# Attention, then two MLPs, in one kernel: q, k and v loaded by whole tiles of tokens, and the attention weights transposed in quarters of the array

## The chip, the cores and the metric

The kernel runs on one core of one Trainium2 chip. The metric is device time in microseconds (us), as the median of several runs. The profile is of one execution.

## The reference

For 8 batches, 8 heads, 576 tokens and a head dimension of 64, attention is computed inside chunks of 64 tokens: scores = q k^T / 8, a softmax over the 64 keys of the chunk, times v. The result, 4608 tokens by 512, goes through two MLPs one after the other:

```python
out = np.matmul(attn, v_c)                     # per (batch, head, chunk of 64 tokens)
x = out.transpose(0, 2, 1, 3).reshape(B * S, H * D)      # 4608 x 512
r = np.maximum(x @ w_in1, 0.0);  x = (r * r) @ w_out1    # 512 -> 2048 -> 512
h = x @ w_in2
g = np.where(h >= 1, h, np.where(h <= -1, 0.0, (h + 1) ** 2 / 4))
return (g @ w_out2).astype(np.float32)
```

q, k and v are float32, the four weight matrices float64.

## The kernel before, in words

A *tile of tokens* is 128 tokens, two chunks; there are 36. A *unit* is half of a tile's heads (HU = 4 heads, as NP = 2 pairs); there are 72 units, two to a tile (UT = 2). The steps of a unit u are functions of their own:

- `load_qk(u)` loads q and k of the unit into one `qkn`, from four buffers in turn (QB = 4). A tile that straddles two batches (4 of 36) needs two DMAs where others need one. `load_v(t)` loads v of a whole tile into one of two `vt` with four DMAs: for each chunk c, the even and the odd heads separately, so that the keys of even heads lie on partitions 0 to 63 and those of odd heads on 64 to 127.
- `att_a` transposes q and k on TensorE into `psA` (four 128x128 transposes), `att_ae` copies them to `qkT` on ScalarE.
- `att_b` makes the scores in `psB`, eight 64x64 matmuls. Rows of the array follow the head's parity e, output partitions follow the chunk c, and the two parities write into two banks of PSUM. Then VectorE takes the row maxima `m` and multiplies them by minus the scale. `att_exp` is four activations on ScalarE with that bias and scale; they also sum up into `z`. `att_n` inverts `z` on VectorE and multiplies on GpSimd.
- `att_c` transposes the weights `s` into `psC` (two 128x128 transposes), `att_ce` copies them to `atT` on ScalarE.
- `att_d` multiplies with v into `psD`, eight 64x64 matmuls whose rows and whose output partitions both follow e, so two quarters of the array are used. `att_x` splits the result into a high part `xh` (ScalarE) and the rest `xl` (VectorE), each in two pieces of 64 partitions.

A float32 matmul stands in the profile as two records (eight matmuls are 16), a float32 transpose as one.

The order of every engine is written out by hand. The *head* is 11 turns, `head(i)`, in which TensorE does attention only: unit i's `att_a`, unit i-1's `att_b`, i-2's `att_c`, i-3's `att_d`. In the turns of DEC a piece of `w_in1` is decoded from float64 as well (`decode`, with `stage_piece` as its load and `bits`, `piece_a` to `piece_c`). After the head, slots follow: `plain_h`, the first matmul of MLP 1 (`ph`), takes 288 slots of six 128x512 matmuls each, and a turn of attention is spread over four slots: `att_d`, `att_b` and `att_x` behind the first, `att_exp` behind the second, `att_c`, `att_ce` and `att_n` behind the third, `att_a`, `att_ae` and the loads behind the fourth. Each two slots yield a `g`, which GpSimd squares and the SP queue stores in two DMAs. Beside this the other three weight matrices are decoded, in 48 units of one per 5.1 slots (`stage_unit`, `unit_a` to `unit_d`): two loads and two stores for most of them, and four sums on GpSimd (`sums`), so that a block of weights becomes the seven combinations of Strassen's method (`wd`, index CIDX). All DMAs are issued by SP, in the program's order.

From slot 288 on come three stretches of 280 slots with the remaining matrix products (`form_b`, `form_a`, line L454 of `products`). The last 16 units of weights are finished there (`late_a` to `late_d`).

Of the kernel before, what the change touches and what calls it, by code (L numbers as in the profile page):

```python
# [15 lines left out]
P = 128  # L16

TINY = 2.0**-15 * 1.125
CH = 64
# [7 lines left out]
CIDX = {"P4": 0, "P1": 1, "P2": 2, "P5": 3, "P6": 4, "P7": 5, "P3": 6}  # L27
# [4 lines left out]
def chunk_attention_moe_moe2(ctx, tc, q, k, v, w_in1, w_out1, w_in2, w_out2, out):  # L32
# [125 lines left out]
    def stage_unit(m, a, b):  # L158
        t = ep.tile([P, 4 * P, 2], U32, tag="ws", name="wu", bufs=2)
        w = (w_out1, w_in2, w_out2)[m]  # L160
        if m == 1:
            src = w.rearrange("(kh kt p) f -> kt p kh f", kh=2, kt=2)[b]
            cols = [(a + fh * HF) * 2 * P for fh in (1, 0)]
        else:
            src = w.rearrange("(kh kk p) d -> kk p kh d", kh=2, kk=HF)[a]
            cols = [(2 * dh + b) * 2 * P for dh in (1, 0)]
        for i, c in enumerate(cols):
            nc.sync.dma_start(
                out=t[:, 2 * i * P:2 * (i + 1) * P].rearrange("p (h f) w -> p h (f w)", h=2),
                in_=src[:, :, c:c + 2 * P],  # L170
            )
        wst[m, a, b] = t
# [8 lines left out]
    def sums(c):  # L181

        for o, x, z, op in ((4, 0, 1, ALU.add), (6, 2, 0, ALU.subtract), (5, 4, 2, ALU.subtract), (7, 3, 5, ALU.subtract)):
            nc.gpsimd.tensor_tensor(out=c[:, o], in0=c[:, x], in1=c[:, z], op=op)
# [5 lines left out]
    def unit_b(m, a, b):  # L190
        y, ab = wst[m, a, b]
        if m == 2:
            c = ep.tile([P, 4, P], F32, tag="wl", name="wq", bufs=2, padded_shape=[P, 7, P])
        else:
            c = ep.tile([P, 8, P], F32, tag="wc", name="wc", bufs=1)
# [10 lines left out]
    def unit_c(*u):  # L206
        c = wst[u]
        hi = ep.tile([P, 7, P], F32R, tag="wh", name="wh", bufs=2)
        nc.scalar.copy(hi, c[:, 1:8])
        wst[u] = (c, hi)  # L210
# [4 lines left out]
    def unit_d(m, a, b):  # L215
        c, hi = wst.pop((m, a, b))
        lo = ep.tile([P, 7, P], F32R, tag="wl", name="wl", bufs=2)
        nc.vector.tensor_tensor(out=lo, in0=c[:, 1:8], in1=f(hi), op=ALU.subtract)
        nc.sync.dma_start(out=wd[m, a][:, 1, b], in_=f(lo))


    def late_a(a, b):
        c = mp.tile([P, 8, P], F32, tag=f"q{LATE[0]}", name="lc")
# [6 lines left out]
    def late_c(a, b):  # L230
        c = wst[a, b]
        hi = mp.tile([P, 7, P], F32R, tag=f"q{LATE[1]}", name="lh", padded_shape=[P, 8, P])
        nc.scalar.copy(hi, c[:, 1:8])
        wst[a, b] = (c, hi)

    def late_d(a, b):
        c, hi = wst.pop((a, b))
        nc.gpsimd.tensor_tensor(out=c[:, 1:8], in0=c[:, 1:8], in1=f(hi), op=ALU.subtract)
        store_parts(2, a, b, hi, c[:, 1:8])
# [27 lines left out]
    def load_qk(u):  # L267
        runs, h0 = runs_of(u // UT), u % UT * HU
        qkn = rt(u % QB, [P, 2, HU, D], "qkn", padded=[P, 2, HU, D])
        for i, src in enumerate((q, k)):  # L270
            for r, n, b, s in runs:
                nc.sync.dma_start(
                    out=qkn[r:r + n, i],
                    in_=src[b, h0:h0 + HU, s:s + n, :].rearrange("h s d -> s h d"),
                )
        att[u] = [qkn]

    def load_v(t):

        for c in range(2):  # L280
            b, s = divmod(2 * t + c, NCB)
            for e in range(2):
                nc.sync.dma_start(
                    out=vt[t % NV][rows(e), c],
                    in_=v[b, e::2, s * CH:(s + 1) * CH, :].rearrange("h s d -> s h d"),
                )

    def att_a(u):

        qkn = att[u][0]  # L290
        pt = pa.tile([P, 2, NP, P], F32, tag="t", name="psA", bufs=2)
        for i in range(2):
            for p in range(NP):
                nc.tensor.transpose(  # L294
                    pt[:, i, p, :], qkn[:, i, 2 * p:2 * p + 2, :].rearrange("p h d -> p (h d)"), ident
# [3 lines left out]
    def att_ae(u):  # L299
        qkT = ep.tile([P, 2, NP, P], F32, tag="qkT", name="qkT", bufs=2)  # L300
        nc.scalar.copy(qkT, att[u])
        att[u] = qkT

    def att_b(u):
# [16 lines left out]
        nc.vector.tensor_reduce(out=m, in_=sc, op=ALU.max, axis=AX.X)  # L321
        nc.vector.tensor_scalar_mul(m, m, -SCALE)
        att[u] = [sc, m, z]

    def att_exp(u):
        sc, m, z = att[u]
        s = ep.tile([P, NP, 2, CH], F32, tag="s", name="s", bufs=2)
        for p in range(NP):
            for e in range(2):
# [5 lines left out]
                    scale=SCALE,  # L335
# [12 lines left out]
    def att_c(u):  # L348
        s, _ = att[u]
        pt = pa.tile([P, NP, P], F32, tag="t", name="psC", padded_shape=[P, HU, P], bufs=2)  # L350
        for p in range(NP):
            nc.tensor.transpose(pt[:, p, :], s[:, p].rearrange("q e k -> q (e k)"), ident)  # L352
        att[u] = pt

    def att_ce(u):
        at = ep.tile([P, NP, P], F32, tag="atT", name="atT", bufs=2)
# [3 lines left out]
    def att_d(u):  # L360
# [3 lines left out]
        for p in range(NP):  # L364
            for c in range(2):
                for e in range(2):
                    nc.tensor.matmul(  # L367
                        pt[rows(e), e, p * P + c * CH:p * P + (c + 1) * CH],
                        vt[u // UT % NV][rows(e), c, u % UT * NP + p, :],
                        at[rows(e), p, rows(c)],  # L370
# [5 lines left out]
    def att_x(u):  # L376
        pt = att.pop(u)
        (xh, xl), a, n = unit_x(u)[0]
        o = [pt[rows(e), e, 0:NP * P].rearrange("d (p t) -> d p t", p=NP) for e in range(2)]
        for e in range(2):  # L380
            nc.scalar.copy(xh[rows(e)], o[e])
        for e in range(2):
            nc.vector.tensor_tensor(out=xl[rows(e)], in0=o[e], in1=f(xh[rows(e)]), op=ALU.subtract)
# [235 lines left out]
    QB = 4  # L619
# [34 lines left out]
    with tc.manual_schedule():  # L654
# [5 lines left out]
        vt = [ep.tile([P, 2, H // 2, D], F32, name=f"vt{i}") for i in range(NV)]  # L660
        load_qk(0)
        make_identity(nc, ident)
        nc.vector.memset(half, 0.5)
        load_qk(1)
        load_qk(2)
        for p in range(2):
            stage_piece(p)
        load_qk(3)
# [19 lines left out]
        def turn(i):  # L688
# [18 lines left out]
            if i + QB < NU:  # L707
                res[3].append((load_qk, (i + QB,)))
# [7 lines left out]
        def head(i):  # L716
# [17 lines left out]
            load_qk(i + QB)  # L734
# [169 lines left out]
```

## Time and profile before

| what | value |
|---|---|
| median of 3 runs | 1670.05 us (1668.27 to 1672.38) |
| the profiled execution | 1671.81 us, its span 1670.0 us |
| TensorE busy | 1613.6 us (97% of the span) |
| VectorE, ScalarE, GpSimd busy | 1140.2, 891.8, 420.3 us (68%, 53%, 25%) |
| DMA queue of SP | 337.74 MB, 67.2% of 16 DMA engines' time |
| the chain of work that ended last | 79% TensorE, 7% VectorE, 7% DMA |

Matmuls are pipelined and overlap in the records, so TensorE's busy time is no sum of durations: the distance from one start to the next says what a matmul costs. The chain follows the work back from the last instruction, each step to what released it. PE is TensorE, PEld its load of weights, DVE VectorE, ACT ScalarE, POOL GpSimd, SP the engine that issues DMAs (SPq).

### The profile page before, as it was taken

The page shows a single profiled execution, that of the slowest core. Times are in us where ns is not written, and L with a number is a line of the kernel's source. Part 1 is how long each engine was busy: PE and PEld are TensorE (multiplying, and loading weights), DVE is VectorE, ACT ScalarE, POOL GpSimd, SP SyncE. Part 2 cuts the span into 40 slices and gives each one's busy share as a digit, 9 for nine tenths or more (in the row PEclk, how much of TensorE's full clock was granted, in tenths as well). Part 3 has the DMA queues.
Part 4 walks back from the last instruction along what each step waited for, and adds up shares of the span by engine and source line. Part 5 has one row for each costly group of instructions (what it writes and reads, how often), then busy time and mean ns, then how long its engine had stood idle before and what let it go on. Part 6 is the DMA issues. An engine that isn't in the chain of part 4 may idle for free.

```text
span 1670.0 us, 27722 instructions
## 1 busy us (share of the span) xinstructions
PE 1613.6 (97%) x9504; PEld 1384.6 (83%) x9504; DVE 1140.2 (68%) x1576; ACT 891.8 (53%) x1852; POOL 420.3 (25%) x466
## 2 busy tenths in 40 slices
PE   6889999999999999999999999999999999999998
PEld 4667777777777889999888898988888899998887
DVE  6967666666645267677677757667574778777776
ACT  6656666666555244444444566666665544444442
POOL 2546565556433410000000234344240000000000
PEclk9999999999999999999999999999999999999999
DMA  7667888888888897335277864655659963654723
GB/s 186 185 183 227 266 267 275 263 271 276 254 254 262 265 290 237 98 123 174 72 230 208 247 229 162 240 173 181 227 201 340 306 188 82 161 140 103 200 40 48
DMA packets 445645, 339.51 MB, mean 203 GB/s; under 512 B 217152, under 2 KB 421952, under 8 KB 445504
## 3 DMA queue, kind: packets, MB, share of 16 engines
q1 hardware_dynamic: 445504, 337.74, 67.2%
q8 instruction: 75, 1.23, 0.3%
q14 instruction: 66, 0.54, 0.1%
HBM read 195.04 MB, written 142.61 MB: 202 GB/s over the span
## 4 chain that ended last, share of the span: by engine, by line
PE 79%; DVE 7%; DMA 7%; issue 3%; ACT 2%; POOL 1%; SPq 1%; POOLq 0%; DVEq 0%; ACTq 0%
PE X L454 31%; PE ph L412 19%; PE V L454 17%; PE W L454 7%; DMA vt<-in_v_dram 2%; PE psD L367 2%; DMA wu<-in_moe_w_out_dram 1%; PE psB L311 1%; PE psA L294 1%; DVE wy L115 1%; DMA ws<-in_moe_w_in_dram 1%; DVE ol L444 1%; DVE wy L118 1%; PE psC L352 1%; DVE t L535 1%
## 5 line engine op out<-in xcount | busy, mean ns | idle before, releaser
L454 PE MATMUL X<-oh,w 128*128 128x448 f32 (+1 forms) x1920 | 557.8, 371 | 5.1 <-DVE c L515 5.0
L443 ACT CAST oh<-gr 128x896 fp32r<-128x896 f32 (+1 forms) x280 | 270.0, 964 | 335.0 <-PE X L454 158.1
L444 DVE TENSOR_TENSOR ol<-gr,oh 128x896 fp32r<-128x896 f32 (+1 forms) x280 | 314.4, 1124 | 182.1 <-ACT oh L443 173.4
L454 PEld LDWEIGHTS X<-oh,w 128*128 128x128 f32 x1920 | 360.0, 188 | 48.2 <-ACT t L529 4.3
L454 PE MATMUL X<-ol,w 128*128 128x448 f32 (+1 forms) x960 | 356.7, 372 | 6.4 <-POOL ol L444 5.2
L454 PE MATMUL V<-oh,w 128*128 128x448 f32 (+1 forms) x960 | 278.5, 371 | 0.0
L412 PE MATMUL ph<-xh,ih 128*128 128x512 f32 x576 | 246.5, 428 | 0.2 <-ACT g L424 0.2
L412 PE MATMUL ph<-xl,ih 128*128 128x512 f32 x576 | 228.9, 397 | 0.0
L412 PE MATMUL ph<-xh,il 128*128 128x512 f32 x576 | 228.8, 397 | 0.0
L425 POOL TENSOR_TENSOR g<-g 128x512 f32<-128x512 f32 x144 | 169.6, 1178 | 158.2 <-ACT g L424 148.8
L454 PEld LDWEIGHTS X<-ol,w 128*128 128x128 f32 x960 | 180.1, 188 | 29.7 <-POOL ol L444 6.8
L454 PEld LDWEIGHTS V<-oh,w 128*128 128x128 f32 x960 | 180.2, 188 | 20.9
L448 DVE TENSOR_TENSOR gr<-gr,gr 128x896 f32<-128x896 f32 (+1 forms) x160 | 177.8, 1111 | 3.6 <-DMA gr<-g 3.6
L454 PE MATMUL V<-ol,w 128*128 128x448 f32 (+1 forms) x480 | 178.0, 371 | 0.0
L424 ACT ACTIVATE g<-ph 128x512 f32<-128x512 f32 x144 | 86.5, 601 | 110.7 <-PE ph L412 100.5
L454 PE MATMUL W<-oh,w 128*128 128x448 f32 (+1 forms) x480 | 139.4, 371 | 0.0
L412 PEld LDWEIGHTS ph<-xl,ih 128*128 128x128 f32 x576 | 109.9, 191 | 25.0
L412 PEld LDWEIGHTS ph<-xh,ih 128*128 128x128 f32 x576 | 109.9, 191 | 22.3 <-ACT g L424 0.5
L444 POOL TENSOR_TENSOR ol<-xr,oh 128x896 fp32r<-128x896 f32 (+1 forms) x15 | 36.5, 2434 | 363.2 <-ACT oh L443 352.1
L412 PEld LDWEIGHTS ph<-xh,il 128*128 128x128 f32 x576 | 110.6, 192 | 16.9
L529 ACT ACTIVATE t<-c,half 128x448 f32<-128x448 f32 (+1 forms) x120 | 81.2, 681 | 71.2 <-DVE c L515 71.0
L535 DVE SCALAR_TENSOR_TENSOR t<-c,t 128x448 f32<-128x448 f32 (+1 forms) x120 | 93.1, 802 | 17.6 <-ACT t L529 17.4
(69 smaller groups left out, 2014.2 us busy)
## 6 DMA issues: line engine op xcount, KB each, us to landing
w<-w SPq DMA_DIRECT2D x168, 256.0 KB, 5.2
gr<-g SPq DMA_DIRECT2D x96, 448.0 KB, 5.1
gr<-g SPq DMA_DIRECT2D x64, 480.0 KB, 4.6
g<-t SPq DMA_DIRECT2D x96, 224.0 KB, 2.6
wu<-in_moe_w_out_dram SPq DMA_DIRECT2D x64, 256.0 KB, 4.8
g<-t SPq DMA_DIRECT2D x64, 240.0 KB, 5.0
w<-wh SPq DMA_DIRECT2D x32, 448.0 KB, 3.8
w<-wl SPq DMA_DIRECT2D x32, 448.0 KB, 4.7
```

The lines of the kernel that those rows point to most:

```text
L115: nc.vector.scalar_tensor_tensor(out=y, in0=w1, scalar=0xC0000000, in1=y, op0=ALU.bitwise_and, op1=ALU.bitwise_or)
L118: nc.vector.scalar_tensor_tensor(out=y, in0=w0, scalar=29, in1=y, op0=ALU.logical_shift_right, op1=ALU.bitwise_or)
L367: nc.tensor.matmul(pt[rows(e), e, p * P + c * CH:p * P + (c + 1) * CH], vt[u // UT % NV][rows(e), c, u % UT * NP + p, :], at[rows(e), p, r ...
L412: nc.tensor.matmul(ph, win[fi][wi][:, kt * P:(kt + 1) * P], x[:, i, :], start=(kt == 0 and a == 0), stop=(kt == KT - 1 and a == 2),)
L424: nc.scalar.activation(out=g, in_=ph, func=AF.Relu)
L425: nc.gpsimd.tensor_tensor(out=g, in0=g, in1=g, op=ALU.mult)
L443: nc.scalar.copy(hi, raw)
L444: eng.tensor_tensor(out=lo, in0=raw, in1=f(hi), op=ALU.subtract)
L448: eng.tensor_tensor(out=o, in0=x, in1=z, op=ALU.subtract)
L454: nc.tensor.matmul(o, wt_[:, wi, c, :], x[:, i, :], start=first and a == 0, stop=last and a == 2, skip_group_check=True,)
L529: nc.scalar.activation(out=t, in_=h, func=AF.Square, bias=half, scale=0.5)
L535: nc.vector.scalar_tensor_tensor(out=t, in0=h, scalar=1.0, in1=t, op0=ALU.max, op1=ALU.min)
```

## The change

q and k are loaded for a whole tile, each into a tile of its own, from two pairs of buffers (QB now counts tiles); the first tile in halves. The load of tile t+2 stands behind the second unit of tile t. v is loaded as it lies, tokens on partitions, with one DMA (two where the tile straddles batches). Attention's weights are transposed by matmuls against a quarter of the identity, chunk by chunk, into one tile of PSUM; then in `att_d` the rows follow the chunk c, the output partitions the parity e, and the two chunks write into two banks. `att_x` takes the result in one piece. The scale is applied to q in its copy, so the copy to `qkT` is in two instructions, and the maximum is negated on its way out. The seven combinations of weights lie in another order, in a tile of seven and not eight parts. At the start the first weights' pieces stand between the loads of the first two tiles.

```diff
-CIDX = {"P4": 0, "P1": 1, "P2": 2, "P5": 3, "P6": 4, "P7": 5, "P3": 6}
+CIDX = {"P1": 0, "P2": 1, "P7": 2, "P4": 3, "P5": 4, "P6": 5, "P3": 6}
...
-        for o, x, z, op in ((4, 0, 1, ALU.add), (6, 2, 0, ALU.subtract), (5, 4, 2, ALU.subtract), (7, 3, 5, ALU.subtract)):
+        for o, x, z, op in ((4, 2, 3, ALU.add), (2, 0, 2, ALU.subtract), (5, 4, 0, ALU.subtract), (6, 1, 5, ALU.subtract)):
...
-        nc.scalar.copy(hi, c[:, 1:8])
+        nc.scalar.copy(hi, c)
...
-    def load_qk(u):
-        runs, h0 = runs_of(u // UT), u % UT * HU
-        qkn = rt(u % QB, [P, 2, HU, D], "qkn", padded=[P, 2, HU, D])
-        for i, src in enumerate((q, k)):
-            for r, n, b, s in runs:
-                nc.sync.dma_start(
-                    out=qkn[r:r + n, i],
-                    in_=src[b, h0:h0 + HU, s:s + n, :].rearrange("h s d -> s h d"),
-                )
-        att[u] = [qkn]
+    qks = {}
+
+    def load_qk(t):
+
+        qks[t] = [rt(2 * (t % 2) + i, [P, H, D], "qkn", padded=[P, H, D]) for i in range(2)]
+        for h0 in range(0, H, HU if t == 0 else H):
+            hs_ = slice(h0, h0 + HU if t == 0 else H)
+            for i, src in enumerate((q, k)):
+                for r, n, b, s in runs_of(t):
+                    nc.sync.dma_start(
+                        out=qks[t][i][r:r + n, hs_],
+                        in_=src[b, hs_, s:s + n, :].rearrange("h s d -> s h d"),
+                    )
 
     def load_v(t):
-
-        for c in range(2):
-            b, s = divmod(2 * t + c, NCB)
-            for e in range(2):
-                nc.sync.dma_start(
-                    out=vt[t % NV][rows(e), c],
-                    in_=v[b, e::2, s * CH:(s + 1) * CH, :].rearrange("h s d -> s h d"),
-                )
+        for r, n, b, s in runs_of(t):
+            nc.sync.dma_start(out=vt[t % NV][r:r + n], in_=v[b, :, s:s + n, :].rearrange("h s d -> s h d"))
...
-        qkn = att[u][0]
+        qkn, h0 = qks[u // UT], u % UT * HU
         pt = pa.tile([P, 2, NP, P], F32, tag="t", name="psA", bufs=2)
         for i in range(2):
             for p in range(NP):
                 nc.tensor.transpose(
-                    pt[:, i, p, :], qkn[:, i, 2 * p:2 * p + 2, :].rearrange("p h d -> p (h d)"), ident
+                    pt[:, i, p, :], qkn[i][:, h0 + 2 * p:h0 + 2 * p + 2, :].rearrange("p h d -> p (h d)"), ident
                 )
         att[u] = pt
     def att_ae(u):
         qkT = ep.tile([P, 2, NP, P], F32, tag="qkT", name="qkT", bufs=2)
-        nc.scalar.copy(qkT, att[u])
+        nc.scalar.activation(out=qkT[:, 0], in_=att[u][:, 0], func=AF.Copy, scale=SCALE)
+        nc.scalar.copy(qkT[:, 1], att[u][:, 1])
         att[u] = qkT
     def att_b(u):
...
         sc = pt[:, :, 0:NP * CH].rearrange("q e (p k) -> q e p k", p=NP)
         m = ep.tile([P, 2, NP], F32, tag="m", name="m", bufs=3)
         z = ep.tile([P, NP, 2], F32, tag="z", name="z", bufs=3)
-        nc.vector.tensor_reduce(out=m, in_=sc, op=ALU.max, axis=AX.X)
-        nc.vector.tensor_scalar_mul(m, m, -SCALE)
+        nc.vector.tensor_reduce(out=m, in_=sc, op=ALU.max, axis=AX.X, negate=True)
         att[u] = [sc, m, z]
     def att_exp(u):
...
                     in_=sc[:, e, p],
                     func=AF.Exp,
                     bias=m[:, e, p:p + 1],
-                    scale=SCALE,
                     accum_out=z[:, p, e:e + 1],
                 )
         att[u] = [s, z]
...
     def att_c(u):
         s, _ = att[u]
-        pt = pa.tile([P, NP, P], F32, tag="t", name="psC", padded_shape=[P, HU, P], bufs=2)
+        pt = pa.tile([P, NP, 2, CH], F32, tag="t", name="psC", padded_shape=[P, HU, 2, CH], bufs=2)
         for p in range(NP):
-            nc.tensor.transpose(pt[:, p, :], s[:, p].rearrange("q e k -> q (e k)"), ident)
+            for e in range(2):
+                for c in range(2):
+                    nc.tensor.matmul(
+                        pt[rows(c), p, e, :], s[rows(c), p, e, :], ident[rows(c), rows(c)], start=True, stop=True
+                    )
         att[u] = pt
     def att_ce(u):
-        at = ep.tile([P, NP, P], F32, tag="atT", name="atT", bufs=2)
+        at = ep.tile([P, NP, 2, CH], F32, tag="atT", name="atT", bufs=2)
         nc.scalar.copy(at, att[u])
         att[u] = at
...
             for c in range(2):
                 for e in range(2):
                     nc.tensor.matmul(
-                        pt[rows(e), e, p * P + c * CH:p * P + (c + 1) * CH],
-                        vt[u // UT % NV][rows(e), c, u % UT * NP + p, :],
-                        at[rows(e), p, rows(c)],
+                        pt[rows(e), c, p * CH:(p + 1) * CH],
+                        vt[u // UT % NV][rows(c), u % UT * HU + 2 * p + e, :],
+                        at[rows(c), p, e, :],
                         start=True,
                         stop=True,
                     )
...
     def att_x(u):
         pt = att.pop(u)
         (xh, xl), a, n = unit_x(u)[0]
-        o = [pt[rows(e), e, 0:NP * P].rearrange("d (p t) -> d p t", p=NP) for e in range(2)]
-        for e in range(2):
-            nc.scalar.copy(xh[rows(e)], o[e])
-        for e in range(2):
-            nc.vector.tensor_tensor(out=xl[rows(e)], in0=o[e], in1=f(xh[rows(e)]), op=ALU.subtract)
+        o = pt[:, :, 0:NP * CH].rearrange("d c (p t) -> d p c t", p=NP)
+        xh, xl = (x.rearrange("d p (c t) -> d p c t", c=2) for x in (xh, xl))
+        nc.scalar.copy(xh, o)
+        nc.vector.tensor_tensor(out=xl, in0=o, in1=f(xh), op=ALU.subtract)
...
-    QB = 4
+    QB = 2
     NV = 2
     LB, LC, LD, LV = 1, 2, 3, 0
     PER = 4
...
         ident = ep.tile([P, P], F32, name="ident")
         plain = tc.tile_pool(name="plain", bufs=1, space=bass.MemoryType.PSUM)
         pa = plain.__enter__()
-        vt = [ep.tile([P, 2, H // 2, D], F32, name=f"vt{i}") for i in range(NV)]
+        vt = [ep.tile([P, H, D], F32, name=f"vt{i}") for i in range(NV)]
         load_qk(0)
         make_identity(nc, ident)
         nc.vector.memset(half, 0.5)
+        stage_piece(0)
         load_qk(1)
-        load_qk(2)
-        for p in range(2):
-            stage_piece(p)
-        load_qk(3)
+        stage_piece(1)
         strokes = []
...
             put(3, att_ae, i)
             if i >= LV and (i - LV) % UT == 0 and i - LV < NU:
                 res[3].append((load_v, ((i - LV) // UT,)))
-            if i + QB < NU:
-                res[3].append((load_qk, (i + QB,)))
+            if i % UT == UT - 1 and i // UT + QB < NU // UT:
+                res[3].append((load_qk, (i // UT + QB,)))
             return res
         def tiles_until(j):
...
             do(att_n, i - LB)
             if (i - LV) % UT == 0:
                 load_v((i - LV) // UT)
-            load_qk(i + QB)
+            if i % UT == UT - 1:
+                load_qk(i // UT + QB)
         for i in range(n0 + LD):
             head(i)
```

## Rows read from the trace of the kernel before

**Rows 1.** The page's chain of work that ended last, by line.
```profile
PE X L454 31%; PE ph L412 19%; PE V L454 17%; PE W L454 7%; DMA vt<-in_v_dram 2%; PE psD L367 2%; DMA wu<-in_moe_w_out_dram 1%; PE psB L311 1%; PE psA L294 1%; DVE wy L115 1%; DMA ws<-in_moe_w_in_dram 1%; DVE ol L444 1%; DVE wy L118 1%; PE psC L352 1%; DVE t L535 1%
```

**Rows 2.** TensorE over time (start us, us, what): units 10, 26, 35, 36, 71.
```profile
42.84 1.11 PE L294 MATMUL psA<-ident,qkn 128*128 128x128 f32 x4
...
181.90 0.60 PE L294 MATMUL psA<-ident,qkn 128*128 128x128 f32 x4
...
250.77 0.60 PE L294 MATMUL psA<-ident,qkn 128*128 128x128 f32 x4
...
258.00 0.60 PE L294 MATMUL psA<-ident,qkn 128*128 128x128 f32 x4
...
529.62 0.60 PE L294 MATMUL psA<-ident,qkn 128*128 128x128 f32 x4
```

**Rows 3.** The same view, inside a turn without waits.
```profile
252.37 0.40 PE L412 MATMUL ph<-xl,ih 128*128 128x512 f32 x1
...
253.88 0.40 PE L412 MATMUL ph<-xh,il 128*128 128x512 f32 x1
254.11 0.39 PE L412 MATMUL ph<-xl,ih 128*128 128x512 f32 x1
...
256.16 0.39 PE L412 MATMUL ph<-xl,ih 128*128 128x512 f32 x1
256.39 0.38 PE L352 MATMUL psC<-ident,s 128*128 128x128 f32 x2
...
256.84 0.40 PE L412 MATMUL ph<-xh,il 128*128 128x512 f32 x1
```

**Rows 4.** TensorE's waits (us, times, longest): 55 to 182 us; 182 to 530.
```profile
PE psD L367 <- ACT atT L357: 6.9, 5, 3.8
...
PE psD L367 <- DMA vt<-in_v_dram: 9.5, 12, 2.5
```

**Rows 5.** The SP queue's issues in order of time (start us, us, what).
```profile
240.19 2.97 SPq L283 DMA_DIRECT2D vt<-in_v_dram  x4
243.25 0.56 SPq L272 DMA_DIRECT2D qkn<-in_q_dram  x1
...
247.30 0.43 SPq L219 DMA_DIRECT2D w<-wl  x1
```

**Rows 6.** Busy us by stretch: PE, PEld, DVE, ACT, POOL; clock, DMA share, GB/s.
```profile
182.00:530.00 348.00, 335.97 (x2796) 266.95 (x2794) 220.52 (x435) 215.24 (x692) 179.79 (x231) 0.99 0.88 265
```

**Rows 7.** TensorE in order of time at the last unit's `psD`.
```profile
544.88 0.39 PE L412 MATMUL ph<-xl,ih 128*128 128x512 f32 x1
545.20 0.68 PE L367 MATMUL psD<-atT,vt 64*64 64x64 f32 x16
...
546.15 0.39 PE L412 MATMUL ph<-xh,il 128*128 128x512 f32 x1
```

**Rows 8.** Groups by line and shape: count, busy us, mean ns, idle before.
```profile
L383 DVE TENSOR_TENSOR xl<-psD,xh 64x256 fp32r<-64x256 f32 x144 | 60.4, 419 | 5.3 <-ACT xh L381 4.2
...
L381 ACT CAST xh<-psD 64x256 fp32r<-64x256 f32 x144 | 52.8, 367 | 64.8 <-PE psD L367 63.9
...
L301 ACT COPY qkT<-psA 128x512 f32<-128x512 f32 x72 | 42.5, 591 | 2.7 <-PE psA L294 2.7
...
L357 ACT COPY atT<-psC 128x256 f32<-128x256 f32 x72 | 28.1, 391 | 2.4 <-PE psC L352 2.4
...
L322 DVE TENSOR_SCALAR m<-m 128x4 f32<-128x4 f32 x72 | 20.1, 279 | 2.5
```

**Rows 9.** All engines in order of time, one turn of the head.
```profile
25.59 0.70 PE L311 MATMUL psB<-qkT 64*64 64x64 f32 x16
...
26.82 0.76 DVE L322 TENSOR_SCALAR m<-m 128x4 f32<-128x4 f32 x1
...
29.52 0.71 PE L311 MATMUL psB<-qkT 64*64 64x64 f32 x16
```

**Rows 10.** DMA traffic from 300 to 400 us.
```profile
DMA packets 37220, 26.65 MB, mean 266 GB/s; under 512 B 22880, under 2 KB 34643, under 8 KB 37207
```

More of the change, by code (lines that the diff above doesn't have):

```diff
@@ L162, in stage_unit @@
             src = w.rearrange("(kh kt p) f -> kt p kh f", kh=2, kt=2)[b]
-            cols = [(a + fh * HF) * 2 * P for fh in (1, 0)]
+            cols = [(a + fh * HF) * 2 * P for fh in (0, 1)]
         else:
             src = w.rearrange("(kh kk p) d -> kk p kh d", kh=2, kk=HF)[a]
-            cols = [(2 * dh + b) * 2 * P for dh in (1, 0)]
+            cols = [(2 * dh + b) * 2 * P for dh in (0, 1)]
         for i, c in enumerate(cols):
@@ L194, in unit_b @@
         else:
-            c = ep.tile([P, 8, P], F32, tag="wc", name="wc", bufs=1)
+            c = ep.tile([P, 7, P], F32, tag="wc", name="wc", bufs=1)
         nc.vector.scalar_tensor_tensor(
@@ L217, in unit_d @@
         lo = ep.tile([P, 7, P], F32R, tag="wl", name="wl", bufs=2)
-        nc.vector.tensor_tensor(out=lo, in0=c[:, 1:8], in1=f(hi), op=ALU.subtract)
+        nc.vector.tensor_tensor(out=lo, in0=c, in1=f(hi), op=ALU.subtract)
         nc.sync.dma_start(out=wd[m, a][:, 1, b], in_=f(lo))
     def late_a(a, b):
-        c = mp.tile([P, 8, P], F32, tag=f"q{LATE[0]}", name="lc")
+        c = mp.tile([P, 7, P], F32, tag=f"q{LATE[0]}", name="lc", padded_shape=[P, 8, P])
         nc.sync.dma_start(out=c[:, 0:4], in_=wq[a, b])
@@ L232, in late_c @@
         hi = mp.tile([P, 7, P], F32R, tag=f"q{LATE[1]}", name="lh", padded_shape=[P, 8, P])
-        nc.scalar.copy(hi, c[:, 1:8])
+        nc.scalar.copy(hi, c)
         wst[a, b] = (c, hi)
@@ L237, in late_d @@
         c, hi = wst.pop((a, b))
-        nc.gpsimd.tensor_tensor(out=c[:, 1:8], in0=c[:, 1:8], in1=f(hi), op=ALU.subtract)
-        store_parts(2, a, b, hi, c[:, 1:8])
+        nc.gpsimd.tensor_tensor(out=c, in0=c, in1=f(hi), op=ALU.subtract)
+        store_parts(2, a, b, hi, c)
     wt = {}
```

## The prediction

> **What bounds the kernel now.** I read the chain of work that ended last first, then the table by stretches, then TensorE's order of time. The chain [rows 1] is 74% TensorE in its four largest parts alone; the L454 parts (55%) lie behind the attention and are not touched, so they stay. What the change touches ends with the attention's last `psD`, at 546 us [rows 7]. There are three parts to it: a head of 11 turns without `ph` matmuls, then a stretch in which the first weights are decoded (to about 182 us), then a steady one.
>
> In the steady one a turn is four slots, 24 `ph` matmuls, with one unit of attention between them. Where nothing waits, a turn takes 258.00 - 250.77 = 7.23 us [rows 2]. The reader can add it up in TensorE's order of time [rows 3]: a `ph` matmul starts 0.23 us after the one before, so 24 are 5.52 us. From the `ph` before `psC` to the second one after it are 0.68 us where two starts would be 0.46: `psC` (two 128x128 transposes) costs 0.22. In the same way `psD` and `psB` together cost 1.51 - 0.46 = 1.05 us. That leaves 0.44 for `psA`. All of it is TensorE's own order, so what is added to these groups is added to the end.
>
> But turns are longer than this. From unit 26's `psA` to unit 71's lie 529.62 - 181.90 = 347.7 us [rows 2] for 45 turns, which would be 325.4: **22.3 us are waiting**. From unit 10's to unit 26's are 139.1 us for 16 turns, 115.7 without waits: **23.4 us**. The waits' list says for what [rows 4]: in the steady stretch `psD` waits for the load of `vt`; earlier it waits for `atT` from ScalarE.
>
> Why is `vt` late? It is emitted at the end of a turn, nine slots (some 16 us) ahead of its use. The SP queue's order of time shows it: 11 issues from 240.19 to 247.30 us [rows 5], 0.65 us each, with no pause between them. The code asks for 4 loads of v, 4 of q and k, 8 stores of `g` and, at a unit of weights per 5.1 slots, some 6.3 for weights per tile of tokens (8 slots): 22.3 issues x 0.65 = 14.5 us, and two turns without waits are 14.46. So the issuing queue is full, lags, and `vt` pays. The DMA engines themselves are busy to 0.88 in the steady stretch [rows 6]: high, but I take the full queue for the first limit.
>
> **The change, part by part.**
>
> *`psC`, +0.59 us a turn.* Two transposes become eight 64x64 matmuls, 16 records on two quarters that lie across from each other (rows 0 to 63 to outputs 0 to 63, and the other half). No such `psC` is in the trace, but `psD` as it stands has the same 16 records on the same two quarters. Once `psD` stands alone between `ph` matmuls [rows 7]: 546.15 - 544.88 = 1.27, less 0.46, is 0.81 us. I take 0.81 for the new `psC`, against 0.22. Bounds: if it ran like `psB` (16 records, which use all four quarters and add only 1.05 - 0.81 = 0.24 us behind `psD`), it would be 0.81 - 0.24 = 0.57; if the two quarters did not overlap at all, see the rivals. Of the two ends, the nearest row is `psD` itself.
>
> *`psD`, -0.24 us a turn.* Its order over quarters becomes that of `psB`, so its 16 records go from some 0.48 us (twice `psB`'s, an estimate from the same rows) to 0.24. The lower bound of the gain is nothing. The pair becomes 0.81.
>
> Over some 63 turns in slots: 63 x (0.59 - 0.24) = **+22 us** (bounds +7 to +37, without the rival).
>
> *Loads, -18.5 us.* v goes from four issues to one per tile, q and k from four to two (four tiles of 36 straddle two batches and take twice that): 22.3 issues become 17.3, x 0.65 = 11.2 us of 14.5. The new loads have twice or more the pieces; the rows give no price for that, but a 64 KB load of v takes 2.97 / 4 = 0.74 us and a 128 KB one of q 0.56 [rows 5], so size is not what an issue costs. If each new one took 1.1 us (twice 0.56), the sum would be 12.6 us, still under a turn pair. q and k are now asked for three turns ahead and not four; that is 22 us, against the 16 that v has, so I cost it at nothing: the queue's slack hides it, and if the queue stayed full, q and k would be late only after v. So the 22.3 us of waits in the steady stretch should mostly go: -20. The bounds are 0 and -22.3.
>
> What comes in their place: `psB` waits for `qkT`, and ScalarE now writes it in two pieces. A piece of 128x256 is the copy of `atT`, 0.39 us [rows 8], so 0.78 against 0.59; `psB` also comes 0.24 us earlier. I charge 1.5 us for turns in which ScalarE is already late. Together -18.5.
>
> *ScalarE and VectorE.* `att_x` takes one 128x256 piece where it took two of 64x256: ScalarE saves 2 x 0.367 - 0.39 = 0.34, less 0.19 for `qkT`; VectorE saves about 0.42 [rows 8]. The multiplication of `m` (0.28 us mean) is gone, as the maximum is negated on its way out and q is scaled in the copy. That is 0.15 us a turn of ScalarE and 0.70 us of VectorE. In the steady stretch TensorE covers it: nothing. In the stretch with the decode VectorE is the engine that is behind (`atT` waits behind `ih`, which waits for VectorE), so 16 turns x 0.70 = 11 us come off the engine that is late; there the weights' loads are late too and are not helped by VectorE. I take -8 of the 23.4 (bounds 0 and -17).
>
> *The head.* There a turn is a loop: `psB`, maximum, `m`, exponentials, `qkT`, next `psB`; 29.52 - 25.59 = 3.93 us [rows 9]. In this turn the multiplication of `m` took 0.76 us, against 0.28 in the mean [rows 8]. Without it, and with 0.19 more for `qkT`, such a turn loses about 0.5 us; in turns with a decode ScalarE is full and gains 0.15. At the start w_in's first piece is asked for after 512 KB and not after 768, but units 2 and 3 wait for theirs to come behind it. TensorE's own sum in a turn hardly changes there (a longer `psC`, a shorter `psD`). I take **-3.5 us** for 11 turns (bounds +2 and -6).
>
> *The rest at nothing.* The weights' seven parts are placed in another order, in as many instructions of the same size; GpSimd's four sums stay four. These run under TensorE; without that cover a changed order would cost no more either. The two identical streams after the attention stay as they are.
>
> **Sum.** 22 - 18.5 - 8 - 3.5 = -8. The profiled execution took 1671.8 us (span 1670.0), the runs' median is 1670.05, so the execution stands 1.75 us above it. 1671.8 - 8 = 1663.8 for such an execution, 1662 as a median of runs.
>
> **The rivals.**
>
> *A: `psC`'s two quarters take turns (slower).* In the kernel before, the halves of the rows always write into two different banks of PSUM; in the new `psC` both write into one tile of one bank. If this makes them go one at a time, its records take 0.96 us where I have 0.48 (an estimate, twice), `psC` is 1.29 and not 0.81: 63 x 0.48 = +30, so 1692. It decides from the point where `psC` costs over about 0.94 us (8 / 63 = 0.13 above my 0.81). Against it: the halves still write different partitions, and no row here shows such a pair. By the Trainium skill, "TensorEngine Tiling (Array Packing)", section "Restrictions and Gotchas", different row tiles write to different banks and cannot access one bank at the same time; no run here shows it yet. By that rule this rival would be the case.
>
> *B: the loads stay late (slower or same).* If the DMA engines, at 0.88, are what makes `vt` late and not the issuing queue, the steady stretch keeps its 22.3 us: -8 + 20 = +12, so 1682. For it: the share, and that of 37220 packets in 100 us of this stretch 22880 are under 512 bytes [rows 10]; a piece of q, k or v is one head's 256 bytes before and after. Against it: the queue without pauses, which alone explains the lag.
>
> *C: more overlap (faster).* If the new `psC` costs 0.57 like four quarters, 63 x 0.24 = 15 us more come off, 1647.
>
> *D: the early stretch gains nothing,* since late loads of weights set it: +8, 1670, no change.
>
> **Chances.** Forecast 0.50 (its own range 1654 to 1671), A 0.13, B 0.12, C 0.12, D 0.13. Faster by over 0.3% (5 us, about what a measurement of this kernel can tell from no change) means under 1665: about 0.36 of the forecast's 0.50, C, and 0.04 of D: 0.52. Within 0.3%: 0.12 of the forecast, 0.07 of D, 0.03 of B: 0.22. Slower: A, most of B and the rest: 0.26. The range leaves out the far half of A and the far end of C: 1645 to 1686.
>
> **What would show it.** In the profile after: `psC` with 16 records and 0.81 us between `ph` matmuls; `psD` with `psB` 0.81; a turn without waits of 7.23 + 0.35 = 7.58 us; unit 26's to unit 71's `psA` in about 343 us; SP with pauses, and `psD` waiting for `vt` hardly at all; `qkT` in two copies of about 0.39; unit 10's `psA` at about 39.5 us. The prediction is wrong if `psC` takes over 1 us, if `vt` is still awaited, or if ScalarE's longer `qkT` makes `psB` wait in most turns.

## The result, and the profile after

The changed kernel takes **1657.27 us** (median of 4 runs, 1653.88 to 1659.24), the kernel before 1670.76 (4 runs beside it). The ratio is 0.9918, with an interval of 0.9895 to 0.9942: faster by 0.8%. The forecast was 1662 in 1645 to 1686. The span of the profiled execution went from 1670.0 to 1657.4 us, 12.6 less.

First the page's chain of work that ended last, of the kernel after; it answers to [rows 1].

```profile
PE 85%; DVE 6%; DMA 3%; issue 2%; ACT 2%; POOL 1%; SPq 0%; POOLq 0%; DVEq 0%; ACTq 0%
PE X L453 31%; PE ph L411 24%; PE V L453 16%; PE W L453 7%; PE psC L350 2%; PE psA L291 2%; PE psD L367 1%; PE psB L309 1%; DVE ol L443 1%; DVE wy L118 1%; DMA w<-lc 1%; DVE t L534 1%; DVE wy L115 1%; DVE xr L447 1%; DVE wy L147 1%
```

TensorE went from 79% of the chain to 85%, and the load of `vt`, 2% before, is no longer in it. `psC` has 2% where it had 1%: the chain now runs more through TensorE's own work, that which the change made longer included.

TensorE's order of time in the kernel after says how long everything took. The `psA` rows answer to [rows 2] (units 10, 26, 35, 36 and 71), the rows between to [rows 3], those at 531 us to [rows 7].

```profile
36.89 0.66 PE L291 MATMUL psA<-ident,qkn 128*128 128x128 f32 x4
...
173.68 0.60 PE L291 MATMUL psA<-ident,qkn 128*128 128x128 f32 x4
...
242.08 0.60 PE L291 MATMUL psA<-ident,qkn 128*128 128x128 f32 x4
...
243.68 0.40 PE L411 MATMUL ph<-xl,ih 128*128 128x512 f32 x1
244.01 0.46 PE L367 MATMUL psD<-atT,vt 64*64 64x64 f32 x16
244.29 0.41 PE L309 MATMUL psB<-qkT 64*64 64x64 f32 x16
244.63 0.50 PE L411 MATMUL ph<-xh,ih 128*128 128x512 f32 x1
244.97 0.39 PE L411 MATMUL ph<-xh,il 128*128 128x512 f32 x1
...
247.26 0.39 PE L411 MATMUL ph<-xl,ih 128*128 128x512 f32 x1
247.58 0.68 PE L350 MATMUL psC<-ident,s 64*64 64x64 f32 x16
248.19 0.50 PE L411 MATMUL ph<-xh,ih 128*128 128x512 f32 x1
248.53 0.39 PE L411 MATMUL ph<-xh,il 128*128 128x512 f32 x1
...
249.68 0.60 PE L291 MATMUL psA<-ident,qkn 128*128 128x128 f32 x4
...
515.68 0.60 PE L291 MATMUL psA<-ident,qkn 128*128 128x128 f32 x4
...
531.32 0.39 PE L411 MATMUL ph<-xl,ih 128*128 128x512 f32 x1
531.64 0.46 PE L367 MATMUL psD<-atT,vt 64*64 64x64 f32 x16
532.03 0.50 PE L411 MATMUL ph<-xh,ih 128*128 128x512 f32 x1
532.37 0.39 PE L411 MATMUL ph<-xh,il 128*128 128x512 f32 x1
```

Read as [rows 3] were: `psC` now adds 248.53 - 247.26 - 0.46 = 0.81 us (0.22 before), `psD` and `psB` together 244.97 - 243.68 - 0.46 = 0.83 (1.05 before), `psD` alone 532.37 - 531.32 - 0.46 = 0.59 (0.81 before). A turn without waits takes 249.68 - 242.08 = 7.60 us; it took 7.23. And the 45 turns from unit 26 to unit 71 take 515.68 - 173.68 = 342.0 us, which is 45 x 7.60: **no time is left for waits**, where 22.2 us were before. TensorE's list of waits from 182 to 530 us, which answers to the second row of [rows 4], has no row at all. The windows of the kernel after say the same (busy us of PE, PEld, DVE, ACT, POOL; clock, DMA share, GB/s; the first stretch answers to [rows 6]):

```profile
182.00:530.00 348.00, 348.00 (x3472) 267.48 (x3471) 178.59 (x351) 204.78 (x693) 183.82 (x229) 1.00 0.88 265
57.00:66.00 9.00, 9.00 (x80) 6.92 (x79) 7.53 (x15) 5.02 (x17) 4.34 (x4) 0.90 0.79 219
48.00:58.00 10.00, 6.00 (x46) 4.45 (x45) 9.10 (x13) 6.68 (x20) 4.70 (x4) 0.70 0.63 201
```

TensorE is busy for 348.00 of 348.00 us in the first stretch, while the DMA engines carry the same 265 GB/s at the same share of 0.88 as in [rows 6]. So they were not what made `vt` late; the experiments with fewer and with more issues below test this. (The other two windows belong to the stretch with the decode; they are read at the end.) The groups of `att_x` and `qkT` by line and shape (count, busy us, mean ns, idle before), which answer to [rows 8]:

```profile
L382 DVE TENSOR_TENSOR xl<-psD,xh 128x256 fp32r<-128x256 f32 x72 | 29.9, 415 | 5.1 <-ACT xh L381 5.1
...
L298 ACT ACTIVATE qkT<-psA 128x256 f32<-128x256 f32 x72 | 27.6, 383 | 2.6 <-PE psA L291 2.6
L299 ACT COPY qkT<-psA 128x256 f32<-128x256 f32 x72 | 27.1, 377 | 0.0
L381 ACT CAST xh<-psD 128x256 fp32r<-128x256 f32 x72 | 27.1, 376 | 50.4 <-PE psD L367 50.4
```

The two pieces of `qkT` take 0.38 us each (forecast 0.39), 0.17 more together than the one copy did; one piece of 128 partitions of `xh` or `xl` takes what one of 64 took, and there are half as many. The issuing queue looks different: this is the SP queue in order of time in the kernel after, to be held against [rows 5].

```profile
238.07 1.22 SPq L283 DMA_DIRECT2D vt<-in_v_dram  x1
240.47 0.79 SPq L430 DMA_DIRECT2D g<-g  x2
241.36 0.87 SPq L213 DMA_DIRECT2D w<-wh  x1
243.06 0.94 SPq L168 DMA_DIRECT2D wu<-in_moe_w_in_dram  x2
244.92 0.81 SPq L430 DMA_DIRECT2D g<-g  x2
```

Between the end of one row and the start of the next there are now pauses of about a microsecond (239.29 to 240.47, 242.23 to 243.06, 244.00 to 244.92). The same view over the whole stretch from 182 to 530 us, added up (pauses are gaps of over 0.3 us):

| kernel | issues | time in issues and short gaps, us | pauses, us | us per tile of tokens |
|---|---|---|---|---|
| before | 520 | 342.9 | 4.5 | 15.45 |
| after | 411 | 252.9 | 92.8 | 15.20 |

The last column is the time from unit 26's `psA` to unit 71's, over 22.5 tiles. TensorE alone needs 14.47 per tile before and 15.20 after.

Where the 12.6 us came from, stretch by stretch, by the `psA` rows:

| stretch | before, us | after, us | difference | forecast |
|---|---|---|---|---|
| to unit 10 (head) | 42.84 | 36.89 | -5.95 | -3.5 |
| unit 10 to 26 (first weights decoded) | 139.1 | 136.8 | -2.3 | +5.6 - 8 = -2.4 |
| unit 26 to 71 (steady) | 347.7 | 342.0 | -5.7 | +15.75 - 18.5 = -2.75 |
| from unit 71 to the end | 1140.4 | 1141.7 | +1.3 | +0.7 |
| span | 1670.0 | 1657.4 | -12.6 | -8 |

(The forecast's +22 is 0.35 us in each of 63 turns, here 16, 45 and 2 of them.)

### The profile page after: what moved, and what is told of

Its sections match the earlier page's. It is cut to its first block, busy times and chain, and to the rows that moved or that the text cites. A ratio compares the mean times of both kernels' runs of the same rounds, so it can differ in the third digit from the quotient of the medians.

```text
span 1657.4 us, 29362 instructions
## 1 busy us (share of the span) xinstructions
PE 1617.0 (98%) x10512; PEld 1376.6 (83%) x10512; DVE 1077.6 (65%) x1432; ACT 873.8 (53%) x1852; POOL 422.4 (25%) x466
## 4 chain that ended last, share of the span: by engine, by line
PE 85%; DVE 6%; DMA 3%; issue 2%; ACT 2%; POOL 1%; SPq 0%; POOLq 0%; DVEq 0%; ACTq 0%
PE X L453 31%; PE ph L411 24%; PE V L453 16%; PE W L453 7%; PE psC L350 2%; PE psA L291 2%; PE psD L367 1%; PE psB L309 1%; DVE ol L443 1%; DVE wy L118 1%; DMA w<-lc 1%; DVE t L534 1%; DVE wy L115 1%; DVE xr L447 1%; DVE wy L147 1%
## 5 line engine op out<-in xcount | busy, mean ns | idle before, releaser
L319 DVE TENSOR_REDUCE m<-psB 128x4 f32<-128x256 f32 x72 | 30.4, 422 | 124.6 <-PE psB L309 124.6
```

## The experiments

Twelve kernels. Ratios are to the kernel before on the same chip, with 95% intervals. "Waits" below are those of the steady stretch: the time from unit 26's `psA` to unit 71's, less 45 turns without waits of that kernel.

**The loads split again, the rest of the change kept.** The quarters and the one-piece sums stay; v goes back to four DMAs a tile, q and k to four.

```diff
-        for h0 in range(0, H, HU if t == 0 else H):
-            hs_ = slice(h0, h0 + HU if t == 0 else H)
+        for h0 in range(0, H, HU):
+            hs_ = slice(h0, h0 + HU)
...
-        for r, n, b, s in runs_of(t):
-            nc.sync.dma_start(out=vt[t % NV][r:r + n], in_=v[b, :, s:s + n, :].rearrange("h s d -> s h d"))
+        for c in range(2):
+            b, s = divmod(2 * t + c, NCB)
+            for e in range(2):
+                nc.sync.dma_start(
+                    out=vt[t % NV][rows(c), e::2],
+                    in_=v[b, e::2, s * CH:(s + 1) * CH, :].rearrange("h s d -> s h d"),
+                )
```

> The changed kernel with its loads issued as before the change: v in four DMAs per tile, q and k in four; bytes and 256-byte pieces stay. Theory (the full issuing queue made vt late): 22.3 issues x 0.65 = 14.5 us per tile against two turns of 15.2, so the queue is 95% full again, pauses nearly vanish, psD waits for vt in some turns: 1660 to 1672. Rival (the DMA engines or the lighter VectorE are what counts): bytes and VectorE are as in the changed kernel, so 1657 within 3 us and no wait for vt.

Measured: 1669.13 us, ratio 0.9992 [0.9976, 1.0008]. All of the gain is gone. The waits of TensorE from 182 to 530 us in this kernel (us, times, longest):

```profile
PE psD L372 <- DMA vt<-in_v_dram: 4.9, 7, 2.0
```

and its SP queue in order of time, full as in [rows 5]:

```profile
243.18 1.11 SPq L168 DMA_DIRECT2D wu<-in_moe_w_in_dram  x2
244.38 0.52 SPq L219 DMA_DIRECT2D w<-wl  x1
244.99 1.19 SPq L435 DMA_DIRECT2D g<-g  x2
246.27 3.29 SPq L285 DMA_DIRECT2D vt<-in_v_dram  x4
249.65 1.03 SPq L435 DMA_DIRECT2D g<-g  x2
```

A tile takes 15.66 us here and its waits come to 10.4, not to 22. The turn of this kernel is the longer one, 7.60 us, and a slower TensorE gives a full queue more time: of TensorE's 45 x 0.37 = 16.5 us of added work, 11.8 fill time in which the kernel before waited, and against that kernel the stretch rises by 4.7 us only. So what the loads are worth depends on how long a turn is. In the kernel before [rows 2] it was the queue and not TensorE that set the pace.

**The scale alone.** The kernel before, with q scaled in its copy and the maximum negated on its way out.

```diff
-        nc.scalar.copy(qkT, att[u])
+        nc.scalar.activation(out=qkT[:, 0], in_=att[u][:, 0], func=AF.Copy, scale=SCALE)
+        nc.scalar.copy(qkT[:, 1], att[u][:, 1])
...
-        nc.vector.tensor_reduce(out=m, in_=sc, op=ALU.max, axis=AX.X)
-        nc.vector.tensor_scalar_mul(m, m, -SCALE)
+        nc.vector.tensor_reduce(out=m, in_=sc, op=ALU.max, axis=AX.X, negate=True)
```

> The kernel before with only the scale moved: q scaled in its copy (two copies of 128x256 to qkT), maximum negated on its way out, no multiplication of m. Theory: head -2 to -4 us (the loop over m is shorter), decode stretch -2 to -5 (0.28 us a turn less of VectorE), steady stretch unchanged with its 22 us of waits for vt: 1661 to 1667. Rival (VectorE's work is what delays the loads): the waits for vt shrink too, under 1655.

Measured: 1667.35, ratio 0.9975 [0.9962, 0.9988]. Unit 10's `psA` starts at 38.59 us and not at 42.84: the head alone gets 4.25 us shorter. The next 16 turns take 135.9 us against 139.1; the steady stretch keeps its waits (23.1 us). The head gained a little more than expected, and the total lies just above the expected range.

**q and k by tile alone,** and with the scale. The first takes `load_qk` and the order of the first loads from the change, and leaves v in four DMAs and `psC` in two transposes; the second adds the edit just shown.

```diff
-    def load_qk(u):
...
+    def load_qk(t):
+
+        qks[t] = [rt(2 * (t % 2) + i, [P, H, D], "qkn", padded=[P, H, D]) for i in range(2)]
...
-    QB = 4
+    QB = 2
```

> The kernel before with only q and k loaded by whole tiles and the start's loads in the new order; v stays in four DMAs, psC and psD as before. Theory: 20.3 issues x 0.65 = 13.2 us per two turns of 14.46, so the queue has pauses and most of the 22 us of waits for vt go, with no cost on TensorE: 1648 to 1656. Rival (DMA engines at 0.88 make vt late, bytes unchanged): waits for vt stay, 1667 to 1671.

> The two before together: the kernel before with q and k by tiles and the scale moved, but transposes, psD and att_x as before. Theory: TensorE keeps turns of 7.23 us, the changed kernel pays 7.60; 63 turns x 0.37 = 23 us less than the changed kernel, less what att_x in one piece gave: 1636 to 1648, under both kernels. Rival (the new psC and psD buy something else that this lacks): no lower than the changed kernel's 1657.

Measured: 1663.87, ratio 0.9959 [0.9943, 0.9976], and 1652.77, ratio 0.9895 [0.9881, 0.9910]. Both missed what I expected (1648 to 1656, and 1636 to 1648), as the steady stretch kept 14.9 and 12.9 us of waits where I had nearly none. TensorE's waits there in the second of the two:

```profile
PE psD L369 <- DMA vt<-in_v_dram: 5.2, 5, 3.0
PE psB L315 <- ACT qkT L305: 0.6, 1, 0.6
```

Two issues fewer per tile should have freed 1.3 us per tile at 0.65 each. But the queue stayed full (pauses 4.7 and 2.3 us of 348), and a tile went from 15.45 to 15.13 and 15.04 us only. The issues that were left took longer: in the first kernel a load of k took 0.74 us in the mean against 0.54, a store of `w` from `wh` 0.66 against 0.44. The load of k now carries twice the bytes, but the store is the same one; and in the changed kernel, whose queue has pauses, the two take 0.65 and 0.69. So **an issue has no fixed price**, and my 0.65 was an average that held for one mix. That the price rises because the queue is behind is not shown.

Still, the second kernel's median is 4.5 us below that of the changed one (their intervals overlap a little), with neither v in one DMA nor the weights in quarters.

**v issued by another engine's queue.** In the kernel before, and in the kernel with q and k by tile and the scale:

```diff
-                nc.sync.dma_start(
+                nc.scalar.dma_start(
                     out=vt[t % NV][rows(e), c],
```

> The kernel before, with the four loads of v per tile issued by ScalarE's queue instead of SP's; number, size and bytes of all DMAs stay. Theory (SP's queue of issues is full): SP has 18.3 issues x 0.65 = 11.9 us per 14.46, so it has pauses, vt is on time and most of the 22 us of waits in the steady stretch go: 1648 to 1656, if ScalarE's own issues (some 2.4 us per two turns, ScalarE is busy 62%) delay nothing. Rival (the DMA engines): 1667 to 1671, waits for vt stay.

> The kernel before with q and k by tiles, the scale moved, and v issued by ScalarE's queue: turns of 7.23 us and, by the theory, no waits in the steady stretch, 12.9 us less than without the other queue: 1637 to 1645, the lowest so far. Rival: v's wait for its buffer at ScalarE's head holds back the exponentials, and psB then waits; not under 1652.

Measured: 1677.66, ratio 1.0039 [1.0022, 1.0056], slower; and 1657.48, ratio 0.9929 [0.9904, 0.9953], no better than without it. Both missed. `vt` is not awaited by `psD` any more, as expected, but waits of other engines from 182 to 530 us in the first of these kernels show what took its place:

```profile
ACT xh L381 <- DMA vt<-in_v_dram: 26.1, 7, 5.8
PE psB L311 <- ACT qkT L301: 10.5, 12, 2.0
```

and these are the waits of its SP queue:

```profile
SPq L431 <- DMA vt<-in_v_dram: 17.7, 16, 2.8
SPq L431 <- POOL g L425: 13.2, 12, 2.7
SPq L219 <- DMA vt<-in_v_dram: 9.0, 5, 3.1
```

ScalarE's own work (`xh`) stands behind the issues of v in its order, so `qkT` is late and `psB` waits for it (10.5 us). And SP, which no longer issues v, waits for v's transfers before stores that do not use them (17.7 us). The trace's records of the issues say why, and it is the kernel's own order: its DMAs use eight semaphores (the counters by which an engine learns that a transfer has landed) in turn, and an issue waits until the DMA that had its semaphore before has landed. A store of `g` issued at 245.10 us has the semaphore of a load of v that was issued at 239.72 and landed at 245.09. In the kernel before, with all issues on SP, these waits come to 1.4 us of the 348, worked out from the landing times; with v on ScalarE's queue they hold SP for 81 us, 35 of them for loads of v, and ScalarE for 17 us for DMAs of SP. So these two kernels do not show what a second queue with semaphores of its own would give.

In the steady stretch both still waited less than without the move (17.7 us against 22.2, and 8.0 against 12.9). The loss lies elsewhere, mostly ahead of it: in the head unit 10 starts at 48.80 us, 6 later than before, and the 16 turns after it take 143.7 us against 139.1; in the second kernel unit 10 starts at 45.23, 7 later than without the move.

**The sums in two pieces again; the old scale again.** Each in the changed kernel.

```diff
-        nc.scalar.copy(xh, o)
-        nc.vector.tensor_tensor(out=xl, in0=o, in1=f(xh), op=ALU.subtract)
+        for e in range(2):
+            nc.scalar.copy(xh[rows(e)], o[rows(e)])
+        for e in range(2):
+            nc.vector.tensor_tensor(out=xl[rows(e)], in0=o[rows(e)], in1=f(xh[rows(e)]), op=ALU.subtract)
```

> The changed kernel with att_x in two pieces of 64 partitions again (0.34 us of ScalarE and 0.42 us of VectorE more per turn). Theory: this is the other part of what lightened the decode stretch and the head: head +1 to +2, decode stretch +2 to +6, steady stretch 0 (TensorE covers it): 1660 to 1666. Rival (the earlier stretch gained from the loads): 1657 within 2.

> The changed kernel with the scale as before (one copy to qkT, m multiplied on VectorE). Theory: the head loses 3 to 5 us, the decode stretch 2 to 4, the steady stretch nothing: 1661 to 1667. Rival (the head gained from the loads' order at the start): head within 2 us of the changed kernel's 36.9.

Measured: 1658.99, ratio 0.9930 [0.9904, 0.9956], and 1659.88, ratio 0.9940 [0.9915, 0.9964]; both within the interval of the changed kernel. By unit 10's `psA` the two pieces cost 1.1 us in the head, the old scale 3.0; in the 16 turns after it 1.4 and 0.7. The head's parts are as expected, but for the decode stretch I had expected 2 to 6 and 2 to 4, so both totals lie below what I expected. The steady stretch is 342.0 us without waits in both, so there ScalarE's and VectorE's work is covered.

**Fewer stores of `g`: the queue relieved in another way.** A `g` of 512 columns that crosses from one half of the tokens to the next was stored in several pieces; with both halves in one buffer a store is one DMA (208 in place of 288). The first kernel adds this to q and k by tile with the scale (v in four DMAs, `psC` in two transposes), the second to the changed kernel.

```diff
-        (w, j, kh, th, kp): dram.tile([P, 2, SIZES[j]], F32, name=f"g{w}_{j}_{kh}{th}{kp}")
+        (w, j, kh, kp): dram.tile([P, 2, 2, SIZES[j]], F32, name=f"g{w}_{j}_{kh}{kp}")
...
-                nc.sync.dma_start(out=gd[0, p, kh, th, kk // 2][:, kk % 2, lo - t0:hi - t0], in_=g[:, lo - b0:hi - b0])
+                nc.sync.dma_start(
+                    out=gd[0, p, kh, kk // 2][:, kk % 2].rearrange("p h n -> p (h n)")[:, lo - t0:hi - t0],
+                    in_=g[:, lo - b0:hi - b0],
+                )
```

> The kernel before with q and k by tiles and the scale moved (1652.8 us), and each g stored in one DMA, or two where it crosses a pair of token blocks (208 issues instead of 288, same bytes). Theory (number of issues fills the queue): some 50 of 488 issues fewer in the steady stretch, SP gets pauses, waits there fall from 12.9 us to under 5: 1641 to 1648. Rival (DMA engines, same bytes): waits stay at 10 or more, 1650 to 1655.

> The changed kernel with the same fewer stores of g. Theory: its queue already has 93 us of pauses in the steady stretch and nothing waits there, so no change: 1657 within 3. Rival: the fewer stores help wherever they are, 1650 or less.

Measured: **1642.29** (1638.62 to 1645.53), ratio 0.9830 [0.9811, 0.9849], and 1657.22, ratio 0.9917 [0.9901, 0.9933]. Both as expected: relieving the queue is worth 10 us where it is full, and nothing where it has pauses. The first is the best of all kernels here and beats both the kernel before and the changed one. The windows of the first and of the second, and then the SP queue of the first, still nearly full (19.4 us of pauses) but no longer behind:

```profile
182.00:530.00 348.00, 347.96 (x2912) 277.59 (x2911) 228.11 (x408) 224.77 (x750) 192.41 (x236) 1.00 0.91 277
182.00:530.00 348.00, 348.00 (x3456) 267.44 (x3456) 177.57 (x349) 204.23 (x691) 183.32 (x229) 1.00 0.87 265
```

```profile
235.35 3.82 SPq L286 DMA_DIRECT2D vt<-in_v_dram  x4
239.26 1.02 SPq L434 DMA_DIRECT2D g<-g  x2
240.38 0.40 SPq L213 DMA_DIRECT2D w<-wh  x1
```

In the first TensorE is busy for 347.96 of 348 us, its turn is the old 7.23, and the 45 turns take 325.9 us against 342.0. The DMA engines move 277 GB/s, against 265 and 271 in this stretch of the kernels before and with q, k and scale, where `vt` was late. The two kernels of this pair were run side by side, and both have q and k by tile, the scale and the merged stores: what separates them, 15 us, is the quarters with v in one DMA, the sums in one piece and the weights' other order. The steady stretch alone holds 342.0 - 325.9 = 16.1 of it, and the quarters' 45 x 0.37 = 16.5 us is that size. No run changes the weights' order alone.

**v one turn earlier.** The kernel before, and the best one, with three buffers for v and its load one turn ahead.

```diff
-    NV = 2
-    LB, LC, LD, LV = 1, 2, 3, 0
+    NV = 3
+    LB, LC, LD, LV = 1, 2, 3, -1
...
+        load_v(0)
```

> The kernel before with a third vt and v asked for one turn earlier; number and order of all other loads stay. If only v's deadline is too tight: the 22 us of waits go, 1647 to 1653. If the queue is over-full (22.3 issues, 14.7 us, per 14.46): it lags further, other loads (weights, and through ScalarE atT and qkT) become late in v's place, 1655 to 1668.

> The kernel before with q and k by tiles, the scale moved, fewer stores of g and v one turn earlier: no waits in the steady stretch, 45 turns of 7.23 us in 326 us, head and decode stretch as with the scale moved: 1636 to 1643, under both kernels. Rival: weights' loads late in v's place, over 1648.

Measured: 1668.32, ratio 0.9984 [0.9972, 0.9996], and 1645.12, ratio 0.9848 [0.9832, 0.9865]. If v had only been asked for too late, the first would have gained most of the 22 us. Its waits of TensorE from 182 to 530 us:

```profile
PE psB L311 <- ACT qkT L301: 4.7, 6, 2.2
PE psD L367 <- ACT atT L357: 2.6, 2, 2.0
```

TensorE no longer waits for `vt`, but for other things: the steady waits are 11.3 us where they were 22.2, in the profiled execution, and the median gains 2 us (the profiled one, 1664.19, is at the low end of its ten runs). The median lies at the upper end of what I expected of an over-full queue, 1655 to 1668. So half of the waits could be moved away from v, and the queue made something else late instead. In the best kernel nothing was left to gain in the steady stretch (325.5 us against 325.9), and the earlier v lengthens what lies ahead of it: unit 10 starts 0.9 us later, and the 16 turns after it take 140.2 us against 135.1. I had expected 1636 to 1643, and it missed.

## Why the prediction was right, by its steps

**`psC` +0.59, `psD` -0.24: right.** 0.81 us against 0.81 for `psC` (+0.59), 0.59 against 0.81 for `psD` (-0.22), 0.83 against 1.05 for the pair, 7.60 against 7.58 for the turn.

**Rival A is out.** `psC`'s two row halves write into one bank and run side by side: 16 records in 0.68 us (247.58), the same as those of the old `psD` into two banks, 0.68 [rows 7]. In both the records start in pairs 7 ns apart, from the second pair on one pair every 58 ns. By the Trainium skill, "TensorEngine Tiling (Array Packing)", section "Restrictions and Gotchas", different row tiles cannot access one bank at the same time. This trace does not agree where the halves write different partitions, and by that rule the time would have been 1692. Rival C is out as well: at 0.81 the two quarters cost what two quarters did in `psD`, not the 0.57 of four. A `psC` over four quarters would have two row halves write the same partitions of a bank; it wasn't tried.

**Loads -18.5: the mechanism right, the size low.** The waits that I counted are time of turns: TensorE's list [rows 4] has 9.5 us for `vt`, its rows together 12.0, and what the other 10 of the 22 consist of I did not itemise. The queue has pauses: 348 / 15.20 = 22.9 tiles have 411 issues, 18.0 each (forecast 17.3), and they take 252.9 / 22.9 = 11.05 us (forecast 11.2). All 22.2 us of waits went; the charge of 1.5 for `qkT` did not come due, as `psB` waits for nothing there. The split loads bring the waits for `vt` back; Rival B is out, since the DMA engines were at 0.88 before and after, and at 0.91 without any wait in the best kernel. SP was not held by landings either (1.4 us, see v on the other queue). What the working did not have: the cost on TensorE and the gain on the queue are not two terms that add up. Before, a tile took 15.45 us because of the queue, after it takes the 15.20 of TensorE; the difference, 5.7 us over the 22.5 tiles, is all that the steady stretch gains. The queue's pace is not a hard limit either: with the same issues and v asked for earlier a tile took 336.8 / 22.5 = 14.97 us in the profiled execution. Why some issues take longer than others of their kind, these runs don't settle. (By the forecast's own terms the stretch would have been 347.7 + 15.75 - 18.5 = 345 us and unit 10's `psA` at 39.3; the 343 and 39.5 written among its signs do not follow from them.)

**Decode stretch, +5.6 - 8 = -2.4: the sum right by luck, the reason not.** Measured -2.3, and the waits in these 16 turns fell from 23.3 to 15.2, the 8 that I forecast. But I gave them to a lighter VectorE, and the single edits don't bear that out: the scale alone gains 3.2, and putting the scale or the two pieces back costs 0.7 and 1.4, while the changed kernel with and without merged stores stands 2 us apart there (134.8 and 136.8). What shows instead is that this stretch is not paced by TensorE: all twelve kernels take 135 to 144 us there, at a turn of 7.23 or of 7.60, where TensorE alone would need 115.7 or 121.6. So I read most of the 8 as TensorE's own added work (16 x 0.37 = 5.9 us) filling time in which it had waited; no run tests that by itself. How much of the rest is VectorE's stays open, as it is near that scatter. Rival D, that nothing is gained there but 5.6 lost, did not come either: the loss was as covered as the gain.

**Head -3.5: under-sized.** Measured -5.95, at the end of its bounds (+2 and -6). The single edits give the scale 3.0 to 4.25, the sums in one piece 1.1, and the loads and their order 0.5 to 1.15, together 4.6 to 6.5. I had charged the loop with 0.19 us for the longer `qkT` and given 0.15 to turns with a decode; with the scale alone a turn lost 4.25 / 11 = 0.39 us in the mean of all eleven.

**The total.** 8 us were forecast and 12.6 came: 2.95 more than forecast in the steady stretch and 2.45 more in the head, 0.1 less in the decode stretch and 0.6 less after unit 71.

## What to carry to other kernels

When an in-order queue is full, its stretch runs at the queue's pace: compare that pace per tile with the engine's own, since a slower engine costs little up to it (4.7 of 16.5 us here) and a relieved queue gains nothing beyond the engine's. Count what else the queue carries before paying on the busiest engine for fewer loads: here merging the stores of `g` freed the queue at no cost on TensorE, and v's layout cost 0.37 us a turn for the same. Do not price an issue by a mean taken from one mix of issues. Before moving issues to another engine, look at the work that stands behind them there and at the semaphores that the two queues share.

## What was not expected of the hardware

- Quarter matmuls from two row halves into one bank of PSUM, each on its own partitions, cost what they cost into two (0.68 us for 16 records either way).
- After TensorE stood still for about 4 us it ran slower for a while. In order of time in the kernel after:

```profile
48.81 0.40 PE L411 MATMUL ph<-xl,ih 128*128 128x512 f32 x1
52.88 0.70 PE L367 MATMUL psD<-atT,vt 64*64 64x64 f32 x16 [3.67 <-ACT atT L357]
53.91 0.71 PE L309 MATMUL psB<-qkT 64*64 64x64 f32 x16 [0.33 <-ACT qkT L299]
54.55 0.79 PE L411 MATMUL ph<-xh,ih 128*128 128x512 f32 x1
55.14 0.63 PE L411 MATMUL ph<-xh,il 128*128 128x512 f32 x1
55.56 0.63 PE L411 MATMUL ph<-xl,ih 128*128 128x512 f32 x1
...
58.55 0.51 PE L411 MATMUL ph<-xh,ih 128*128 128x512 f32 x1
```

  The `ph` matmuls then start 0.43 us apart and not 0.23, and `psB` takes 0.71 where it takes 0.41 at full clock: TensorE is at the lower of its levels, 1.2 GHz. The granted clock of the two windows shown above is 0.70 and 0.90, and from 52.0 to 58.8 us alone it is 0.50. Eight `ph` from 55.14 to 58.55 us take 3.41 us where they would take 1.84 at 0.23 each, so some 1.6 us are lost there after the stop of 3.67 us.
- The whole-tile load of v took 0.41 us to issue (median of 24 in the steady stretch), less than one of the four quarter loads before it, 0.60 (median of 88), though it carries four times the bytes: size did not set the price of an issue. Nor did form alone: whole-tile loads of q and of k, of one form, took 0.41 and 0.65 (medians of 23 each).
